# First tile's scores and row maxima ahead of the branch, row sums in PSUM, and a new order: windowed attention with two MoE layers on one core

## Chip, cores and metric

One core of a Trainium2 chip runs the whole program. The metric is device time in microseconds (us) of one execution. TensorE (the matmul engine) is PE in the profile, VectorE is DVE, ScalarE is ACT, GpSimd is POOL, SyncE is SP.

## What is computed

Sixteen attention heads (2 batches of 8; 768 rows, 64 wide) with 4 sink columns and a window of 128, then two feed-forward layers on the 1536 x 512 result.

```
scores = q @ k.T / sqrt(D)
keep = is_sink | in_window
a = exp(where(keep, scores, -1e9) - row max); a = a / (sum(a) + 1e-9)
x = a @ v
h = x @ w_in;  g = where(h >= 1, h, where(h <= -1, 0, (h + 1)**2 / 4));  x = g @ w_out
x = sigmoid(x @ w_gate) * (x @ w_val) @ w_out2
```

Sinks and window are inputs, so the program has two arms: a banded one for sizes that fit (these do), and a dense one for the rest. The arm is taken by a branch on a flag that the engines load into registers.

## The kernel before

Attention goes by tiles of 112 query rows, 7 per batch, 14 in all; each tile has four slots of two heads. Every slot takes the steps of `slot` in `banded`: PE makes the scores of both heads into a PSUM bank (`scores`, L922); DVE adds the mask and takes the row maximum in one custom instruction (`top`, L925); ACT takes the exponential and, with an accumulator read after it, the row sum (`exp`, L931); PE transposes the result (`turn`, L939); ACT or DVE copies it to SBUF as pts (`take`, helper line L353 or L355); PE multiplies with v (`values`, L962), all four slots of a tile together, into one bank. At the end of a tile DVE adds 1e-9 to the sums and inverts them (`inverse`, L976 and L977), the inverse is widened into ie, PE spreads it by four transposes (`spread`, L985), and the product is written as a high and a low float32r half (xh and xl) for the MoE layers. The first tile of a batch has only 128 key columns, the others 256.

The MoE matmuls are three per product (high by high, high by low, low by high): L550 to L552 for the first layer's input side, L595 to L597 for its output side, L712 and L798 to L800 for the second layer. Their weights arrive as int64 pieces through st, are put together by ACT and DVE (w), and split into halves.

A planner (`Plan.order`) sets the order of every engine's queue: it takes steps with costs, due times (`SLOT_DUE`, `FINISH`, `MOE_DUE` and others) and biases, and appends on each engine the step that is due first among those that can run. `Plan.fillers` puts matmuls of the identity (`fill`, L349) where it expects PE to stand idle in the first 55 us. The order is fixed when the program is built.

Ahead of the branch, in `moe_chain_kernel`: SP loads the sizes (nw) and the first tile's q and k, ACT issues the loads of its v and loads its exponential table (L1203); PE runs six warm matmuls (L1208); POOL tests the sizes (`banded_test`, its last step L1106 writes the flag); DVE makes the first mask. All engines then read the flag (L1212, L1213). The second tile's q and k are asked for behind the branch (L874).

The DMA loads take turns on eight semaphores: a load that reuses one waits, on the queue that issues it, until the load that used it before has landed.

Of the kernel before, what the change touches and what calls it, by code (L numbers as in the profile page):

```python
# [11 lines left out]
F32 = mybir.dt.float32  # L12
# [6 lines left out]
P = 128  # L19
# [33 lines left out]
START = {"DVE": 0.2}  # L53

BIAS = {"DVE": 0.31, "POOL": -0.06, "ACT": -0.05}

SLOT_DUE = 2.36

FINISH = {"top": 8.3, "exp": 5.74, "turn": 12.73, "pts": 8.44, "values": -10.81, "div": 8.03, "out": -13.31}
MOE_DUE = 62.74  # L60
MOE_PACE = 3.69
DRAIN = 1.91
EARLY = 18.59
LATE = 15.13
# [4 lines left out]
FIRST_TOPS = 4  # L69
SAME_MODE = 5.77  # L70
# [61 lines left out]

class Op:
# [3 lines left out]
class Plan:  # L137
# [40 lines left out]
    def order(self):  # L178
# [12 lines left out]
        done, events, now, order, mode = 0, [0.0], 0.0, [], None  # L191
# [106 lines left out]
class Body:  # L298


    def __init__(self, ctx, tc, a, out, pre):
# [17 lines left out]
        self.banks = [None] * 8  # L319
# [48 lines left out]

    def open_banks(self):
        ps = self.pool(self.ctx, "ps", True)  # L370
        self.psum = [ps.tile([P, 512], F32, name=f"bank{i}") for i in range(len(self.banks))]
# [467 lines left out]
    def banded(self):  # L839
# [3 lines left out]
        self.open_banks()  # L843
# [21 lines left out]
        def slot(k, due):  # L865
# [19 lines left out]
            if t == 0:  # L885
                v, rv = (lambda: first), cells("acc", 0, c0 - P, c0)
                op("SP", 0.0, -99.0, lambda: None, [], rq, lat=0.0)
                op("SP", 0.0, -99.0, lambda: None, [], rv, lat=2.0 + 0.2 * p)
# [8 lines left out]
            if j == 0:  # L897
                sc = [Buf(sc_r) for _ in range(2)]
# [3 lines left out]
            pr, mx, pt, pts = Buf(pr_r), Buf(mx_r), Buf(pt_r), Buf(pts_r)  # L902
# [21 lines left out]
            def top(e):  # L924
                nc.vector.tensor_tensor_reduce(  # L925
                    out=pr.ap[:n, e, :ks * P], in0=banks[e].ap[:n, j, :ks * P], in1=mask[:n, :ks * P], op0=ALU.add, op1=ALU.min,
                    scale=-0.125, scalar=3.0e38, accum_out=mx.ap[:n, e:e + 1],
                )
# [13 lines left out]
            yield 0.43 * f, scores, rq, [(x, j) for x in sc], sc  # L942
            for e in range(2):
                tops.append(op("DVE", d2_us(m) + 0.01, due - FINISH["top"], lambda e=e: top(e), [(banks[e], j), ("mask", min(i, 2))], [(pr, e), (mx, e)], uses=[banks[e], pr, mx]))
            for e in range(2):
                op("ACT", a_us(m) + 0.185, due - FINISH["exp"], lambda e=e: exp(e), [(mx, e)], [(pr, e), (sums, 2 * p + e)], uses=[pr, mx, sums])
            op("PE", 0.38 * f + 0.02, due - FINISH["turn"], turn, [(pr, 0), (pr, 1)], [pt], uses=[pr])

# [20 lines left out]
            if p == NP - 1:  # L969
# [22 lines left out]
                op("DVE", 0.28, due - FINISH["div"], inverse, [(sm, h) for h in range(H)], [sm], port=True)  # L992
# [16 lines left out]
        for k in range(0, len(slots), NP):  # L1009
            if k == NP:  # L1010
                op("DVE", 1.25, SLOT_DUE * (NP - 2), masks.make_second, [], [("mask", 1)], after=tops[:FIRST_TOPS])
# [3 lines left out]
            for j in range(0, NP, SCORES_OF):  # L1015
# [12 lines left out]
    def dense(self):  # L1028
# [5 lines left out]
        with ExitStack() as ctx:  # L1034
            ap, pp = self.pool(ctx, "dense"), self.pool(ctx, "dps", True)
            t = lambda shape, tag, dt=F32: ap.tile(shape, dt, tag=tag, name=tag)
            for b, p in [(b, p) for b in range(self.B) for p in range(NP)]:
# [5 lines left out]
                for i in range(S // P):  # L1043
# [11 lines left out]
                    ot = pp.tile([P, P], F32, tag="ot", name="ot")  # L1055
                    for e in range(2):
                        es = slice(64 * e, 64 * e + 64)
                        sc = pp.tile([P, 2, 512], F32, tag="sc", name="sc")
                        for c in range(2):
                            cs = slice(c * half, (c + 1) * half)  # L1060
                            for n, (x, y) in enumerate(((qh, kh), (qh, kl), (ql, kh))):
                                nc.tensor.matmul(out=sc[:, c, :half], lhsT=x[es, :], rhs=y[es, cs], start=n == 0, stop=n == 2)
                        pr, sm = t([P, S], "pr"), t([P, 4], "sm")
                        for c in range(2):
                            cs = slice(c * half, (c + 1) * half)
                            nc.vector.scalar_tensor_tensor(out=pr[:, cs], in0=sc[:, c, :half], scalar=0.125, in1=keep[:, cs], op0=ALU.mult, op1=ALU.mult)
# [7 lines left out]
                        pt, pts = pp.tile([P, 8, P], F32, tag="pt", name="pt"), t([P, nk, P], "pts")  # L1074
                        for c in range(nk):
                            nc.tensor.transpose(out=pt[:, c, :], in_=pr[:, c * P:(c + 1) * P], identity=ident)
                        nc.scalar.activation(out=pts, in_=pt[:, :nk, :], func=AF.Copy)
# [4 lines left out]
        self.open_banks()  # L1082

    def split(self, v, hi, lo):
        self.nc.scalar.activation(out=hi, in_=v, func=AF.Copy)
        self.nc.vector.tensor_tensor(out=lo, in0=v, in1=f32v(hi), op=ALU.subtract)


def banded_test(nc, const, nf):
# [10 lines left out]
    banded = const.tile([1, 1], F32, name="banded")  # L1100
# [20 lines left out]
class Masks:  # L1121
# [27 lines left out]
    def make_first(self):  # L1149
# [4 lines left out]
        self.weigh(m0)  # L1154
# [10 lines left out]
    def make_others(self):  # L1165
# [3 lines left out]
        v.tensor_copy(out=even[:, P:], in_=odd[:, :P])  # L1169


@with_exitstack
def moe_chain_kernel(ctx: ExitStack, tc: tile.TileContext, a, out):
# [12 lines left out]
    with tc.manual_schedule():  # L1186
# [18 lines left out]
        with tc.tile_pool(name="warm", bufs=1, space=bass.MemoryType.PSUM) as warm:  # L1205
            w = warm.tile([P, P], F32, name="warm")
            for i in range(WARM):
                nc.tensor.matmul(out=w, lhsT=pre["ident"], rhs=pre["ident"], start=i == 0, stop=i == WARM - 1)  # L1208
        pre["masks"] = Masks(nc, const, nf, pre["acc"])
        banded = banded_test(nc, const, nf)  # L1210
        pre["masks"].make_first()
        on = nc.values_load(banded[0:1, 0:1], min_val=0, max_val=0x3F800000)  # L1212
    with tc.If(on > 0) as branch:  # L1213
# [77 lines left out]
```

## Time and profile before

| | |
|---|---|
| median of 3 runs | 631.98 us (631.81 to 632.01) |
| profiled execution | 631.99 us |
| its span, first to last instruction | 630.2 us |
| busy: PE, DVE, ACT, POOL | 620.8, 498.8, 320.6, 160.1 us |
| mean granted clock of PE, share of full | 0.996 |

The profiled execution lies within 0.01 us of the median. Busy times are sums over stages with different limits, so the stretches have to be read apart: attention up to about 116 us, the first MoE layer mixed into it and after it, then the second. Matmuls overlap, and a busy PE may be busy with filler matmuls.

### The profile page before, as it was taken

How to read it: one execution, taken by the hardware profiler on the slowest of the kernel's cores; microseconds unless marked ns; L12 is line 12 of the kernel's file. 1: busy time of each engine (PE TensorE's matmuls, PEld its weight loads, DVE VectorE, ACT ScalarE, POOL GpSimd, SP SyncE). 2: the span in 40 equal slices, each digit the busy share in tenths (PEclk: the TensorE clock that was granted, in tenths of full speed). 3: DMA queues.
4: the chain of work that ended last, by engine and by line, in shares of the span. 5: the costliest groups of instructions: out<-in, count | busy, mean ns of one | idle time of the engine just before them, and what ended most of it. 6: DMA issues, size and time to landing. Idle time of an engine off the chain costs nothing.

```text
span 630.2 us, 9870 instructions
## 1 busy us (share of the span) xinstructions
PE 620.8 (99%) x3540; PEld 541.9 (86%) x3540; DVE 498.8 (79%) x1034; ACT 320.6 (51%) x736; POOL 160.1 (25%) x187
## 2 busy tenths in 40 slices
PE   7999999999999999999999999999999999999996
PEld 6778878888888888888888999998998998998995
DVE  4999998699996984459967697599789789786373
ACT  5999999646532531134435565663353442541430
POOL 1113411312000130025142323252351361460100
PEclk8999999999999999999999999999999999999999
DMA  6785655142441210001300001221212202200004
GB/s 186 255 260 179 177 174 185 47 153 82 154 147 67 70 65 33 1 0 34 124 11 0 1 34 67 101 68 67 100 36 71 97 34 100 69 1 0 1 35 172
DMA packets 28571, 54.48 MB, mean 86 GB/s; under 512 B 3296, under 2 KB 18400, under 8 KB 28512
## 3 DMA queue, kind: packets, MB, share of 16 engines
q1 hardware_dynamic: 27936, 53.49, 25.6%
q8 instruction: 30, 0.49, 0.3%
q10 hardware_dynamic: 576, 0.26, 0.1%
q14 instruction: 29, 0.24, 0.1%
HBM read 50.60 MB, written 3.15 MB: 85 GB/s over the span
## 4 chain that ended last, share of the span: by engine, by line
PE 95%; DVE 3%; DMA 1%; issue 0%; POOL 0%; ACT 0%
PE bank L712 28%; PE bank L550 7%; PE bank L595 7%; PE bank L596 7%; PE bank L597 7%; PE bank L551 7%; PE bank L552 7%; PE bank L800 5%; PE bank L799 5%; PE bank L798 5%; PE bank L922 3%; PE bank L962 3%; PE bank L939 3%; DVE pr L925 1%; PE bank L349 1%; PE bank L985 1%
## 5 line engine op out<-in xcount | busy, mean ns | idle before, releaser
L712 PE MATMUL bank<-xh,early 128*128 128x384 f32 x384 | 108.2, 334 | 0.0
L712 PE MATMUL bank<-late,early 128*128 128x384 f32 x432 | 85.5, 335 | 0.0
L712 PEld LDWEIGHTS bank<-late,early 128*128 128x128 f32 x432 | 76.1, 188 | 0.6
L712 PEld LDWEIGHTS bank<-xh,early 128*128 128x128 f32 x384 | 70.3, 188 | 0.4
L353 ACT ACTIVATE early<-w 128x512 fp32r<-128x512 f32 (+1 forms) x52 | 30.2, 582 | 68.5 <-PE bank L800 28.1
L712 PE MATMUL bank<-xl,early 128*128 128x384 f32 x192 | 64.2, 334 | 0.0
L808 DVE TENSOR_TENSOR acc<-bank,acc 128x512 f32<-128x512 f32 (+1 forms) x61 | 41.6, 681 | 21.5 <-PE bank L800 21.0
L569 ACT ACTIVATE tmp<-tmp 128x512 f32<-128x512 f32 x48 | 30.0, 629 | 52.2 <-DVE tmp L566 52.2
L931 ACT ACTIVATE pr<-pr,mx 112x256 f32<-112x256 f32 (+2 forms) x112 | 54.0, 488 | 4.3 <-DVE mx L925 4.2
L465 DVE SCALAR_TENSOR_TENSOR w<-st,w 128x512 int32<-128x512 int32 x68 | 51.0, 753 | 0.3
L462 DVE SCALAR_TENSOR_TENSOR w<-st,w 128x512 int32<-128x512 int32 x68 | 50.4, 743 | 0.8
L611 DVE TENSOR_TENSOR acc<-bank,acc 128x512 f32<-128x512 f32 x36 | 24.4, 688 | 29.1 <-PE bank L597 29.1
L405 POOL TENSOR_TENSOR w<-w 128x256 f32<-128x256 f32 x48 | 41.5, 876 | 21.7 <-DVE w L465 11.1
L566 DVE TENSOR_SCALAR tmp<-bank 128x512 f32<-128x512 f32 x48 | 32.7, 686 | 13.3 <-PE bank L552 12.8
L451 ACT ACTIVATE w<-st 128x512 f32<-128x512 f32 x60 | 39.3, 663 | 6.7 <-DMA st<-in_w 2.5
L353 ACT ACTIVATE gs<-tmp 128x512 fp32r<-128x512 f32 (+1 forms) x49 | 30.3, 621 | 23.7 <-DVE tmp L572 22.2
L925 DVE CUSTOM_DVE_ANT_0 pr<-bank,mask 112x256 f32<-112x256 f32 (+2 forms) x112 | 39.2, 396 | 3.6 <-PE bank L922 3.3
L360 DVE TENSOR_TENSOR early<-w,early 128x512 fp32r<-128x512 f32 x45 | 33.9, 758 | 7.4 <-POOL early L357 6.3
L456 DVE TENSOR_SCALAR w<-w 128x512 f32<-128x512 f32 x68 | 35.6, 526 | 5.2 <-ACT w L451 5.2
L360 POOL TENSOR_TENSOR early<-w,early 128x512 fp32r<-128x512 f32 (+1 forms) x25 | 27.0, 1083 | 46.7 <-ACT early L353 34.3
L550 PE MATMUL bank<-xh,early 128*128 128x512 f32 x96 | 38.3, 399 | 0.3 <-DVE mx L925 0.3
L595 PE MATMUL bank<-gs,early 128*128 128x512 f32 x96 | 38.0, 396 | 0.0
(170 smaller groups left out, 1557.1 us busy)
## 6 DMA issues: line engine op xcount, KB each, us to landing
st<-in_w SPq DMA_DIRECT2D x32, 512.0 KB, 3.3
v<-in_vb SPq DMA_DIRECT2D x52, 128.0 KB, 2.9
qk<-in_qk SPq DMA_DIRECT2D x48, 128.0 KB, 3.2
st<-in_wg SPq DMA_DIRECT2D x12, 512.0 KB, 3.3
st<-in_wv SPq DMA_DIRECT2D x12, 512.0 KB, 3.3
st<-in_wo SPq DMA_DIRECT2D x12, 512.0 KB, 3.2
out<-acc SPq DMA_DIRECT2D x11, 256.0 KB, 2.1
acc<-in_qk SPq DMA_DIRECT2D x12, 128.0 KB, 3.1
```

Source lines behind the costliest of these rows:

```text
L353: self.nc.scalar.activation(out=out, in_=x, func=AF.Copy)
L360: (self.nc.vector if e == "DVE" else self.nc.gpsimd).tensor_tensor(out=out, in0=x, in1=y, op=ALU.subtract)
L462: nc.vector.scalar_tensor_tensor(out=t(), in0=high(), scalar=-0x80000000, in1=t(), op0=ALU.bitwise_and, op1=ALU.bitwise_or)
L465: nc.vector.scalar_tensor_tensor(out=t(), in0=low(), scalar=29, in1=t(), op0=ALU.logical_shift_right, op1=ALU.bitwise_or)
L550: mm(out=out, lhsT=wh[:, c], rhs=mh, start=k == 0, stop=False)
L551: mm(out=out, lhsT=wh[:, c], rhs=ml, start=False, stop=False)
L552: mm(out=out, lhsT=wl[:, c], rhs=mh, start=False, stop=k == KD - 1)
L595: mm(out=out, lhsT=wh[:, c], rhs=gh, start=f == fs[0], stop=False)
L596: mm(out=out, lhsT=wh[:, c], rhs=gl, start=False, stop=False)
L712: nc.tensor.matmul(out=out, lhsT=w[:, c], rhs=m, start=start and i == n == 0, stop=i == 1 and n == 2, skip_group_check=True)
L925: nc.vector.tensor_tensor_reduce(out=pr.ap[:n, e, :ks * P], in0=banks[e].ap[:n, j, :ks * P], in1=mask[:n, :ks * P], op0=ALU.add, op1=ALU.m ...
L931: nc.scalar.activation(out=pr.ap[:n, e, :ks * P], in_=pr.ap[:n, e, :ks * P], func=AF.Exp, bias=mx.ap[:n, e:e + 1], scale=-1.0, accum_out=s ...
```

## The change

The program gets eight PSUM banks at its start. Ahead of the branch, PE now makes the scores of the whole first tile (L1244) and DVE its masked rows and maxima (the new helper `row_tops`, L1188), into a free piece of acc and a small tile mx0. The q and k of the first two tiles and the v of the first are loaded ahead of the branch, by SP and ACT in turn. POOL's test ends after two subtractions, and DVE makes the flag from them in one instruction (L1122); the branch compares it with the bit pattern of 1.0. The row sums of the exponentials go into eight spare columns of the bank that later takes the tile's values, and `inverse` reads them there. The planner's numbers are new. In the dense arm, which doesn't run here, the banks are the shared ones; that part and other small edits are left out below.

```diff
-START = {"DVE": 0.2}
+START = {"ACT": 0.9, "DVE": 2.1, "PE": 1.0, "SP": 1.1}
...
-SLOT_DUE = 2.36
+SLOT_DUE = 3.32
...
-SAME_MODE = 5.77
+SAME_MODE = 0.06
...
             if t == 0:
                 v, rv = (lambda: first), cells("acc", 0, c0 - P, c0)
...
-                load(own, src(i), due - 6, held(t) if t < RAW else [mine])
+                if t > 1:
+                    load(own, src(i), due - 6, held(t) if t < RAW else [mine])
...
+            total = lambda o: self.psum[o.bank][:, NP * TQ:NP * TQ + 2 * NP]
 
             def exp(e):
                 nc.scalar.activation(
                     out=pr.ap[:n, e, :ks * P], in_=pr.ap[:n, e, :ks * P], func=AF.Exp,
-                    bias=mx.ap[:n, e:e + 1], scale=-1.0, accum_out=sums.ap[:n, 2 * p + e:2 * p + e + 1],
+                    bias=mx.ap[:n, e:e + 1], scale=-1.0, accum_out=total(o)[:n, 2 * p + e:2 * p + e + 1],
                 )
...
-            yield 0.43 * f, scores, rq, [(x, j) for x in sc], sc
+            if t:
+                yield 0.43 * f, scores, rq, [(x, j) for x in sc], sc
...
-                    nc.vector.tensor_scalar(out=x[:, 1], in0=x[:, 0], scalar1=1e-9, scalar2=None, op0=ALU.add)
+                    nc.vector.tensor_scalar(out=x[:, 1], in0=total(o)[:n], scalar1=1e-9, scalar2=None, op0=ALU.add)
...
-    v.tensor_tensor(out=a, in0=a, in1=b, op=ALU.mult)
-    v.tensor_scalar(out=a, in0=a, scalar1=0.0, scalar2=None, op0=ALU.is_ge)
-    v.tensor_tensor(out=a[:, :2], in0=a[:, :2], in1=a[:, 2:], op=ALU.mult)
-    v.tensor_tensor(out=banded, in0=a[:, :1], in1=a[:, 1:2], op=ALU.mult)
-    return banded.bitcast(I32)
+    return a, b
+
+
+def banded_flag(nc, const, fits):
...
+    nc.vector.tensor_tensor_reduce(out=a, in0=a, in1=b, op0=ALU.mult, op1=ALU.max, scale=-1.0, scalar=0.25, accum_out=flag)
+    return flag.bitcast(I32)
...
+def row_tops(nc, out, x, mask, top):
+    nc.vector.tensor_tensor_reduce(out=out, in0=x, in1=mask, op0=ALU.add, op1=ALU.min, scale=-0.125, scalar=3.0e38, accum_out=top)
...
-        for p in range(min(KD, NP)):
-            c0 = p * NT + S - TQ - 2 * NS
-            nc.sync.dma_start(out=pre["acc"][:, c0:c0 + NQK], in_=a["qk"][0, 0, p])
+        pairs = [(p, p * NT + S - TQ - 2 * NS, (nc.sync, nc.scalar)[p % 2]) for p in range(NP)]
+        for p, c0, queue in pairs:
+            queue.dma_start(out=pre["acc"][:, c0:c0 + NQK], in_=a["qk"][0, 0, p])
+        for p, c0, queue in pairs:
+            queue.dma_start(out=pre["acc"][:, c0 + NQK:c0 + 2 * NQK], in_=a["qk"][0, 1, p])
+        for p, c0, queue in pairs:
             v = pre["acc"][:, c0 - P:c0]
-            nc.scalar.dma_start(out=v, in_=a["vb"][0, 0, p, :, 1])
+            queue.dma_start(out=v, in_=a["vb"][0, 0, p, :, 1])
...
+        masks.make_first()
+        flag = banded_flag(nc, const, fits)
+        masks.weigh(masks.first)
...
+        for p, c0, _ in pairs:
+            for e in range(2):
+                x = pre["acc"][64 * e:64 * e + 64, c0:c0 + NQK]
+                nc.tensor.matmul(out=first[e][:, p], lhsT=x[:, :TQ], rhs=x[:, TQ + NS:], start=True, stop=True)
+        for p in range(NP):
+            for e in range(2):
+                row_tops(nc, rows(p)[:, e], first[e][:, p], masks.first, pre["mx"][:, 2 * p + e:2 * p + e + 1])
+        on = nc.values_load(flag[0:1, 0:1], min_val=0, max_val=0x7F800000)
+    with tc.If(on < FIRST_FLAG) as branch:
```

PE's queue, from the flag on. Before (L922 scores of the first tile, L349 fillers, L939 transposes):

```order
L1212 TENSOR_LOAD banded
L1213 COMPARE_AND_BRANCH
L922 MATMUL bank_160<-acc 112x128
...
L349 MATMUL bank_165<-ident 128x128 x5
L939 MATMUL bank_164<-ident,pr 128x112 x2
L349 MATMUL bank_160<-ident 128x128
L939 MATMUL bank_165<-ident,pr 128x112 x2
L349 MATMUL bank_160<-ident 128x128 x4
L922 MATMUL bank_166<-acc 112x256
```

And now (L1244 scores of the first tile, L927 of the second, L943 transposes, L970 values, L354 fillers, L993 the spread):

```order
L1244 MATMUL bank_98<-acc 112x128
...
L1248 TENSOR_LOAD flag
L1249 COMPARE_AND_BRANCH
L927 MATMUL bank_93<-acc 112x256
...
L943 MATMUL bank_97<-ident,acc 128x112 x2
L943 MATMUL bank_98<-ident,acc 128x112 x2
...
L970 MATMUL bank_92<-pts,acc 64x112 x8
L354 MATMUL bank_93<-ident 128x128 x3
L993 MATMUL bank_99<-ident,ie 128x112 x4
```

The first tile's scores have moved ahead of the flag, the second tile's stand right behind it in one group of eight, and three fillers stand behind the first tile's values. Before, ten stood between the first tile's scores and the second's.

ACT's queue from its start. Before (L931 exponentials, L353 copies):

```order
L1196 DMA acc<-in_vb 128x128 x4
L1203 ACT_TABLE_LOAD
L1203 ACTIVATE scratch<-ident 1x1
L1212 TENSOR_LOAD banded
L1213 COMPARE_AND_BRANCH
L931 ACTIVATE pr,sm<-pr,mx 112x128 x4
L353 ACTIVATE pts<-bank_164 128x2x112
L931 ACTIVATE pr,sm<-pr,mx 112x128
L353 ACTIVATE pts<-bank_165 128x2x112
L931 ACTIVATE pr,sm<-pr,mx 112x128 x3
L353 ACTIVATE ie<-sm 112x512
```

And now (L935 exponentials, L358 copies):

```order
L1213 DMA acc<-in_qk 128x256 x2
L1215 DMA acc<-in_qk 128x256 x2
L1218 DMA acc<-in_vb 128x128 x2
L1225 ACT_TABLE_LOAD
L1225 ACTIVATE scratch<-ident 1x1
L1248 TENSOR_LOAD flag
L1249 COMPARE_AND_BRANCH
L935 ACTIVATE acc,bank_92<-acc,mx_131 112x128 x8
L358 ACTIVATE pts<-bank_97 128x2x112
...
L935 ACTIVATE pr,bank_98<-pr,mx 112x256 x4
```

Two more DMA issues stand ahead of the table load, all eight exponentials of the first tile stand ahead of its four copies of pts, each writes its sum to a bank, and the copy of ie has left this stretch.

PE in two later tiles, before:

```order
L922 MATMUL bank_160<-qk_177 112x256
...
L939 MATMUL bank_165<-ident,pr 128x112 x4
L939 MATMUL bank_163<-ident,pr 128x112 x4
L922 MATMUL bank_166<-qk_185 112x256
...
L985 MATMUL bank_167<-ident,ie 128x112 x4
L939 MATMUL bank_161<-ident,pr 128x112 x4
L962 MATMUL bank_165<-pts,v 64x112 x16
```

And now:

```order
L927 MATMUL bank_92<-qk_198 112x256
...
L927 MATMUL bank_98<-qk_190 112x256
...
L943 MATMUL bank_93<-ident,pr 128x112 x4
L943 MATMUL bank_99<-ident,pr 128x112 x4
L993 MATMUL bank_92<-ident,ie 128x112 x4
L943 MATMUL bank_93<-ident,pr 128x112 x4
L943 MATMUL bank_94<-ident,pr 128x112 x4
L970 MATMUL bank_97<-pts,v 64x112 x16
```

Two groups of four score matmuls, with transposes between them, have become one group of eight, and the spread stands ahead of the values as before. Over the whole attention the order has 20 groups of scores before and 16 behind the branch now.

## Rows read from the trace of the kernel before

**Rows 1.** The page's first part: busy us, share of the span, instructions.

```profile
PE 620.8 (99%) x3540; PEld 541.9 (86%) x3540; DVE 498.8 (79%) x1034; ACT 320.6 (51%) x736; POOL 160.1 (25%) x187
```

**Rows 2.** Windows: stretch, length, busy by engine (instructions), PE clock, DMA share, GB/s.

```profile
20.00:50.00 30.00, 29.74 (x318) 22.93 (x315) 29.78 (x123) 29.61 (x102) 3.96 (x6) 1.00 0.76 247
50.00:100.00 50.00, 49.42 (x468) 40.50 (x468) 49.42 (x161) 47.98 (x155) 15.34 (x18) 1.00 0.61 185
```

**Rows 3.** PE's waits behind its first matmuls: us in total, times, longest.

```profile
PE bank L939 <- DVE mx L925: 0.3, 1, 0.3
PE bank L939 <- ACT pts L353: 0.3, 1, 0.3
PE bank L550 <- DVE mx L925: 0.3, 1, 0.3
```

**Rows 4.** Timeline of PE, 6 to 17 us: start, us, operation, count, idle before.

```profile
6.33 1.13 PE L922 MATMUL bank<-acc 64*112 64x128 f32 x16 [2.05 <-POOL banded L1106]
7.39 2.20 PE L349 MATMUL bank<-ident 128*128 128x128 f32 x10
9.39 0.58 PE L939 MATMUL bank<-ident,pr 112*128 112x112 f32 x2
...
10.59 1.35 PE L349 MATMUL bank<-ident 128*128 128x128 f32 x8
...
13.36 0.40 PE L349 MATMUL bank<-ident 128*128 128x128 f32 x2
13.60 0.55 PE L985 MATMUL bank<-ident,ie 112*128 112x112 f32 x4
14.08 1.12 PE L922 MATMUL bank<-acc 64*112 64x256 f32 x8
...
16.96 1.98 PE L922 MATMUL bank<-acc 64*112 64x256 f32 x16
```

**Rows 5.** Timeline of ACT, SP and POOL (q: the queue issues), to 14 us.

```profile
0.72 1.86 ACTq L1196 DMA_DIRECT2D acc<-in_vb  x4
...
2.62 1.28 ACT L1203 ACT_TABLE_LOAD   x1 [2.62 <-issue]
...
3.86 0.33 SPq L1194 DMA_DIRECT2D acc<-in_qk  x1
...
5.23 0.18 POOL L1106 TENSOR_TENSOR banded<-fits 1x1 f32<-1x1 f32 x1
...
7.53 0.40 ACT L931 ACTIVATE pr<-pr,mx 112x128 f32<-112x128 f32 x1 [3.42 <-DVE mx L925]
7.84 0.18 ACT L931 ACTIVATION_READ_ACCUMULATOR pr<-pr,mx 112x1 f32 x1
7.93 0.39 ACT L931 ACTIVATE pr<-pr,mx 112x128 f32<-112x128 f32 x1
...
13.86 0.51 ACT L931 ACTIVATE pr<-pr,mx 112x256 f32<-112x256 f32 x1
```

**Rows 6.** What SP's queue waited for: us in total, times, longest.

```profile
SPq L1194 <- DMA acc<-in_vb: 1.3, 1, 1.3
```

**Rows 7.** Timeline of DVE: the second mask's first and last step, a maximum.

```profile
8.83 0.28 DVE L1158 TENSOR_SCALAR mask<-acc,nf 112x128 f32<-112x128 f32 x1
...
9.87 0.29 DVE L1147 TENSOR_SCALAR mask<-mask 112x256 f32<-112x256 f32 x1
...
13.02 0.42 DVE L925 CUSTOM_DVE_ANT_0 pr<-bank,mask 112x256 f32<-112x256 f32 x1 [0.24 <-PE bank L922]
```

**Rows 8.** Groups of ACT by form: busy us, mean ns of one, idle before.

```profile
L353 ACT ACTIVATE bank<-bank 128x384 f32<-128x384 f32 x48 | 22.9, 476 | 13.7 <-PE bank L712 13.2
L931 ACT ACTIVATION_READ_ACCUMULATOR pr<-pr,mx 112x1 f32 x96 | 18.6, 194 | 0.0
...
L353 ACT ACTIVATE tmp<-bank 128x384 f32<-128x384 f32 x24 | 11.7, 486 | 7.6 <-PE bank L712 7.4
```

**Rows 9.** Windows again, 8 to 10 us.

```profile
8.00:10.00 2.00, 2.00 (x11) 2.00 (x11) 1.97 (x16) 1.18 (x7) 0.00 (x0) 0.50 0.89 253
```

More of the change, by code (lines that the diff above doesn't have):

```diff
@@ L52 @@
 DMA_LAT = 2.7
-START = {"DVE": 0.2}
-BIAS = {"DVE": 0.31, "POOL": -0.06, "ACT": -0.05}
-SLOT_DUE = 2.36
[L59 to L64, printed above, removed]
+START = {"ACT": 0.9, "DVE": 2.1, "PE": 1.0, "SP": 1.1}
+READY = {"tops": 0.2, "next": 0.5, "values": 1.5}
+BIAS = {"DVE": 0.92, "POOL": 0.54, "ACT": 0.39}
+SLOT_DUE = 3.32
+FINISH = {"top": 3.98, "exp": 6.33, "turn": 10.24, "pts": 21.57, "values": -3.1, "div": -2.85, "out": -20.08}
+MOE_DUE = 126.14
+MOE_PACE = 8.22
+DRAIN = 2.91
+EARLY = 31.49
+LATE = 44.63
 ENTER, LEAVE = {"rows": 0.18, "cols": 0.14}, 0.09
@@ L68 @@
 VALUES_OF = 4
-FIRST_TOPS = 4
-SAME_MODE = 5.77
+SAME_MODE = 0.06
 WARM = 6
@@ L130, in __init__ @@
         ring.asked.append(self)
+class Kept:
+    def __init__(self, ap):
+        self.ap = ap
 class Op:
@@ L190, in order @@
                     ready[e].append((0.0, o))
-        done, events, now, order, mode = 0, [0.0], 0.0, [], None
+        done, events, now, order, mode = 0, sorted({0.0, *START.values()}), 0.0, [], None
         running = []
@@ L924, in top @@
             def top(e):
[L925 to L928, printed above, removed]
+                row_tops(nc, pr.ap[:n, e, :ks * P], banks[e].ap[:n, j, :ks * P], mask[:n, :ks * P], mx.ap[:n, e:e + 1])
+            total = lambda o: self.psum[o.bank][:, NP * TQ:NP * TQ + 2 * NP]
             def exp(e):
@@ L991, in slot @@
                 m = NP * n
-                op("DVE", 0.28, due - FINISH["div"], inverse, [(sm, h) for h in range(H)], [sm], port=True)
+                op("DVE", 0.28, due - FINISH["div"], inverse, [(sm, h) for h in range(H)], [sm], port=True, uses=[o])
                 pool = t >= POOL_FROM
@@ L1010, in banded @@
             if k == NP:
-                op("DVE", 1.25, SLOT_DUE * (NP - 2), masks.make_second, [], [("mask", 1)], after=tops[:FIRST_TOPS])
+                op("DVE", 1.25, SLOT_DUE * (NP - 2), masks.make_second, [], [("mask", 1)])
             if k == 2 * NP:
@@ L1014, in banded @@
             tile = [slot(k + j, SLOT_DUE * (k + j)) for j in range(NP)]
-            for j in range(0, NP, SCORES_OF):
+            for j in range(0, NP if k else 0, SCORES_OF):
                 both(tile[j:j + SCORES_OF], SLOT_DUE * (k + j), "rows")
@@ L1061, in dense @@
                             for n, (x, y) in enumerate(((qh, kh), (qh, kl), (ql, kh))):
-                                nc.tensor.matmul(out=sc[:, c, :half], lhsT=x[es, :], rhs=y[es, cs], start=n == 0, stop=n == 2)
+                                nc.tensor.matmul(out=sc[c][:, :half], lhsT=x[es, :], rhs=y[es, cs], start=n == 0, stop=n == 2)
                         pr, sm = t([P, S], "pr"), t([P, 4], "sm")
@@ L1065, in dense @@
                             cs = slice(c * half, (c + 1) * half)
-                            nc.vector.scalar_tensor_tensor(out=pr[:, cs], in0=sc[:, c, :half], scalar=0.125, in1=keep[:, cs], op0=ALU.mult, op1=ALU.mult)
+                            nc.vector.scalar_tensor_tensor(out=pr[:, cs], in0=sc[c][:, :half], scalar=0.125, in1=keep[:, cs], op0=ALU.mult, op1=ALU.mult)
                         nc.vector.tensor_tensor(out=pr, in0=pr, in1=fill, op=ALU.add)
@@ L1073, in dense @@
                         nc.vector.tensor_scalar(out=pr, in0=pr, scalar1=sm[:, 3:4], scalar2=None, op0=ALU.mult)
-                        pt, pts = pp.tile([P, 8, P], F32, tag="pt", name="pt"), t([P, nk, P], "pts")
+                        pts = t([P, nk, P], "pts")
                         for c in range(nk):
-                            nc.tensor.transpose(out=pt[:, c, :], in_=pr[:, c * P:(c + 1) * P], identity=ident)
-                        nc.scalar.activation(out=pts, in_=pt[:, :nk, :], func=AF.Copy)
+                            x = pt[c // 4][:, c % 4 * P:(c % 4 + 1) * P]
+                            nc.tensor.transpose(out=x, in_=pr[:, c * P:(c + 1) * P], identity=ident)
+                        for c in range(0, nk, 4):
+                            m = min(4, nk - c)
+                            nc.scalar.activation(out=pts[:, c:c + m].rearrange("p c n -> p (c n)"), in_=pt[c // 4][:, :m * P], func=AF.Copy)
                         for c in range(nk):
@@ L1204, in moe_chain_kernel @@
         pre["scratch"] = scratch
[L1205 to L1213, printed above, removed]
+        ps = ctx.enter_context(tc.tile_pool(name="ps", bufs=1, space=bass.MemoryType.PSUM))
+        pre["psum"] = [ps.tile([P, 512], F32, name=f"bank{i}") for i in range(8)]
+        for i in range(WARM):
+            nc.tensor.matmul(out=pre["psum"][0][:, :P], lhsT=pre["ident"], rhs=pre["ident"], start=i == 0, stop=i == WARM - 1)
+        pre["masks"] = masks = Masks(nc, const, nf, pre["acc"])
+        fits = banded_test(nc, const, nf)
+        masks.make_first()
+        flag = banded_flag(nc, const, fits)
+        masks.weigh(masks.first)
+        pre["mx"] = const.tile([TQ, 2 * NP], F32, name="mx0")
+        pre["pr"] = [pairs[p // 2][1] + 3 * NQK + p % 2 * 2 * P for p in range(NP)]
+        rows = lambda p: pre["acc"][:TQ, pre["pr"][p]:pre["pr"][p] + 2 * P].rearrange("p (e n) -> p e n", e=2)
+        pre["rows"] = rows
+        first = [pre["psum"][6 + e][:TQ].rearrange("p (i n) -> p i n", i=NP) for e in range(2)]
+        for p, c0, _ in pairs:
[7 more added lines that the diff above has]
+    with tc.If(on < FIRST_FLAG) as branch:
         with tc.manual_schedule(), ExitStack() as arm:
```

38 lines of the change are left out of this document (20 added, 18 removed).

## The prediction, made before the changed kernel ran

> **What bounds the kernel now.** I read four views in this order. The page's first part [rows 1] has TensorE (PE) busy for 620.8 of 630.2 us, so time can come from two places only: from what PE does that is no work, and from the few us in which it does nothing. The windows by stretch [rows 2] say where the other engines could stop PE: from 20 to 100 us DVE and ACT are as full as PE (ACT 29.6 of 30 us, then 48.0 of 50; DVE 29.8 and 49.4). The list of PE's waits [rows 3] shows how little is lost later: three waits of 0.3 us, 0.9 together. The timeline of PE's first 17 us [rows 4] shows the rest: it stands for 2.05 us before its first matmul behind the branch, and from 7.39 to about 11.9 it does little but filler matmuls (L349, identity by identity), while ACT's exponentials go on and the second tile's q and k, which are asked for only after the branch, are on their way. So the start is a chain through DMA, DVE and ACT that PE covers with fillers; from about 14 us on PE, ACT and DVE are all full; after the attention PE alone counts.
>
> **What the change takes off PE.**
> First, the first tile's scores. Their 16 records run from 6.33 to 7.39 [rows 4], behind the branch; now they stand ahead of it, in time in which PE waited. 1.06 us off.
> Second, fillers. The old order has 13, two records each. Ten records take 2.00 us (7.39 to 9.39), eight 1.35, two 0.24 (13.36 to 13.60) [rows 4]; the six others I put at 0.9. Together 4.5 us. The new order has four: three behind the first tile's values and one later. One costs between 0.24 and 0.40 by the same rows; I take 0.3, 1.2 us. 3.3 us off.
> Third, regrouping. Four score matmuls last 1.12 us and eight last 1.98 [rows 4], so a group of scores costs some 0.2 us beside its work. Without the first tile the old order has 19 such groups and the new one 16; with an estimated 0.1 us for the switch ahead of each, and for each of three switches fewer from MoE matmuls into the attention, 1.2 us are off.
> Fourth, the branch. The flag was POOL's last step, 5.23 to 5.41, and PE's first matmul came 0.92 us later [rows 4, 5]. Now DVE makes it in one step in place of POOL's last four, at about 4.9 us. But PE has scores ahead of its flag read, and their q and k must land: ACT's first load, issued at 0.72, landed when SP's fourth issue could go, at 3.86 [rows 5, 6], so those issued by 1.7 us land up to 4.8. PE is through its scores at about 5.3 and passes the branch at about 6.2, 0.1 us earlier.
> Together 5.7 us.
>
> **What it adds.** Two waits.
> ACT's queue now issues six DMAs where it issued four in 1.86 us, and loads its exponential table behind them (1.28 us) [rows 5]. The fifth and sixth reuse the semaphores of ACT's own first two loads, and SP's fourth issue waited 1.3 us for such a landing [rows 6]. So ACT's fifth goes at about 3.9 us, the sixth ends near 4.8, the table near 6.1, and with the small activation and the branch the first exponential starts at about 6.6, against 7.53 [rows 5]. Eight exponentials of the first tile at 0.39 us and four copies of pts at about 0.25 end at 10.7, where the second tile's exponentials can start: 3.1 us before the 13.86 of now. PE meanwhile does the second tile's scores (6.2 to 8.1) and has then eight transposes and eight values (about 0.8 and 0.9 us) until 11.2. That leaves 1.4 us in which it waits, in place of fillers.
> The values now also wait for DVE: the sums lie in the bank that the values write, and DVE's reading of them must be over first. In the new order it stands behind four maxima of the second tile. DVE ends the first tile's maxima at about 6.9 (at 8.83 now [rows 7]), is through the branch at 7.6, needs 1.3 us for the second mask (8.83 to 10.16) and 1.6 for four maxima of 0.42 at most, and has read the sums by about 10.8: 0.1 us more for PE. In the later tiles PE's spread of the reciprocals mostly stands ahead of the values and waits for a later DVE or POOL step anyway: nothing.
> So 1.5 us come back. The 0.9 us of waits I leave as they are.
>
> **The row sums in PSUM.** No row shows ACT's accumulator written there. Its read lasts 194 ns, and the next exponential starts 0.09 us after the read began (7.84 to 7.93) [rows 5, 8]. The nearest row is a copy of 384 columns that ends in PSUM, 476 ns against 486 into SBUF [rows 8]: 0.01 us off each of 112, 1.1 us of ACT. As one end I take 0.04 us each (four times that row, 4.5 us of ACT); at the other the overlap is lost, 0.10 us more each and 11.2 us of ACT. I take 0.01, by the nearest row. Being ACT time, it pays PE nothing directly; it and seven ie copies fewer on ACT (now DVE's and POOL's) let ACT keep up with a PE that has 5.7 us less to do. The copies moved to POOL I cost at nothing: PE has transposes ahead of the spread. Without that cover PE waits for each.
>
> **The sum.** The profiled execution took 631.99 us (span 630.2 and 1.8 around it); the median of the runs is 631.98. 631.99 - 5.7 + 1.5 = **627.8 us**. With the filler price and the wait in the ramp at their ends, 626.4 to 629.2.
>
> **A rule that speaks against it.** From 8 to 10 us the granted clock was 0.50, that is 1.2 GHz [rows 9], after PE had stood for 2.05 us ahead of its first matmul; after more fillers and work it was 2.4 GHz (1.00 from 20 us on [rows 2]). The change takes fillers out of just this stretch, but fills the hole ahead of the branch in part. The Trainium skill (TensorE: Matmul & The Clock Gate, What's actually happening) says that the throttled state is the default and that activity releases it. By that rule the new wait behind 8.1 us could bring a slow stretch of its own; the rival below gives its time from rows.
>
> **The rivals.**
> *No wait in the ramp.* ACT could read the flag while its table loads and start at 6.0, and the fillers may fall where PE waits. Then the 1.5 us don't come back, and some of the 0.9 goes: 626.0.
> *ACT and DVE set the pace.* Up to the last attention matmul the new order has 36 MoE matmuls fewer on PE to fill in with, and DVE takes over some xl and ie work from POOL and ACT. From 20 to 100 us ACT had 2.4 us to spare and DVE 0.8 [rows 2]. If PE must wait 2 us more for them in the later tiles: 629.8. For it speaks that all three are full, against it the ACT time saved.
> *The clock falls late.* If it is at half from about 11 to 14.5 us, the 2.5 us of values, transposes and scores there take twice as long: 630.3.
> *It doesn't do what it says.* If ACT's queue is another microsecond late and PE's scores wait longer for their landings, the start is as long as now, and the regrouping alone pays 0.3 us: 631.7.
> *Slower: the accumulator.* If a PSUM destination loses the overlap, each exponential takes 0.10 us more, 11.2 us of ACT; behind its 2.4 us of idle time 8.8 us reach PE: 636.6. From 0.07 us each on (7.8 less 2.4 is 5.4, more than the 4.2 gained) it is slower than now. The only row against it is the copy into PSUM, which is no longer than the one into SBUF.
>
> **How the numbers follow.** Forecast 0.48; no wait in the ramp 0.13; ACT and DVE 0.17; clock 0.09; no effect 0.05; slower 0.08. A measurement of this kernel can tell 0.2%, 1.26 us, from no change. Faster by more: all of the first two, 0.14 of the third and 0.07 of the fourth, 0.82. Within it: the rest of these and no effect, 0.10. Slower: 0.08. The range from 625.5 to 630.5 takes in the first two, most of the third and the clock, and leaves out some 0.17.
>
> **What would show it.** Right: PE's first matmul behind the branch near 6.2 us and the second tile's; the first exponential near 6.6, the second tile's near 10.7; four fillers; some 1.5 us of PE waiting for ACT or DVE between 8 and 12 us and about 1 us after that; accumulator reads of about 185 ns; PE's last attention matmul some 12 us earlier than now (4.2 and 36 MoE matmuls). Wrong: accumulator reads that hold up the next exponential by 0.16 us or more, the clock at 0.5 beyond 12 us, or several us of PE waits between 20 and 160 us.

## The result, and the profile after

The changed kernel takes 638.75 us (median of 5 runs), the kernel before 631.98: slower, by a ratio of 1.0118 (95% interval 1.0104 to 1.0132). The forecast was 627.8. Below is the windows view of the changed kernel, in the columns of [rows 2].

```profile
20.00:50.00 30.00, 27.35 (x316) 21.77 (x316) 25.52 (x110) 29.28 (x96) 3.32 (x5) 1.00 0.70 216
50.00:100.00 50.00, 47.64 (x450) 37.25 (x446) 46.07 (x160) 47.09 (x148) 13.77 (x17) 1.00 0.60 184
```

Before, PE, DVE and ACT were about equally full in these 80 us [rows 2]. Now, from 20 to 50 us, ACT alone is: it is busy for 29.28 of 30 us, PE for 27.35 (29.74 before) and DVE for 25.52 (29.78). From 50 to 100 us none of the three is (PE 47.64, ACT 47.09, DVE 46.07 of 50). So PE and DVE wait. PE's list of waits (columns of [rows 3]; its two largest and the next on ACT):

```profile
PE bank L943 <- ACT pts L358: 2.5, 5, 0.6
PE bank L993 <- DVE mx L1188: 1.7, 2, 1.0
...
PE bank L927 <- ACT on L358: 0.5, 1, 0.5
```

What makes ACT full is seen in ACT's timeline (start, us, operation):

```profile
4.76 1.04 ACTq L1218 DMA_DIRECT2D acc<-in_vb  x2
5.84 1.28 ACT L1225 ACT_TABLE_LOAD   x1 [5.84 <-DMA acc<-in_qk]
7.13 0.20 ACT L1225 ACTIVATE scratch<-ident 1x1 f32<-1x1 f32 x1
7.75 0.40 ACT L935 ACTIVATE acc<-acc,mx 112x128 f32<-112x128 f32 x1 [0.42 <-DVE mx L1188]
...
13.29 0.51 ACT L935 ACTIVATE pr<-pr,mx 112x256 f32<-112x256 f32 x1
13.70 0.15 ACT L935 ACTIVATION_READ_ACCUMULATOR pr<-pr,mx 112x1 f32 x1
13.89 0.51 ACT L935 ACTIVATE pr<-pr,mx 112x256 f32<-112x256 f32 x1
14.30 0.15 ACT L935 ACTIVATION_READ_ACCUMULATOR pr<-pr,mx 112x1 f32 x1
14.49 0.51 ACT L935 ACTIVATE pr<-pr,mx 112x256 f32<-112x256 f32 x1
14.90 0.15 ACT L935 ACTIVATION_READ_ACCUMULATOR pr<-pr,mx 112x1 f32 x1
14.96 0.56 ACT L358 ACTIVATE on<-bank 128x448 f32<-128x448 f32 x1
```

The accumulator read lasts 0.15 us where it lasted 0.19 [rows 8], but the exponential behind it starts 0.19 us after the read began (13.70 to 13.89); before it was 0.09 [rows 5]. So the exponential waits until the read has ended. A copy behind a read does not: it starts 0.06 after the read began (14.90 to 14.96). Over the whole trace, from the start of one 256-column exponential to the start of the one directly behind it is 0.599 us now (median of 63) and was 0.492 (median of 54); below this is called the step.

The start is less of a change than forecast. PE's timeline:

```profile
5.25 2.05 PE L1244 MATMUL bank<-acc 64*112 64x128 f32 x16 [0.97 <-DMA acc<-in_qk]
7.09 3.21 PE L927 MATMUL bank<-acc 64*112 64x256 f32 x16
10.23 0.70 PE L943 MATMUL bank<-ident,acc 112*128 112x112 f32 x5
11.22 0.32 PE L943 MATMUL bank<-ident,acc 112*128 112x112 f32 x1 [0.30 <-ACT acc L935]
11.99 0.41 PE L943 MATMUL bank<-ident,acc 112*128 112x112 f32 x2 [0.45 <-ACT pts L358]
```

The first tile's 16 score records stand ahead of the branch, as the change says, but they wait for q and k until 5.25 and take 2.05 us where they took 1.13 [rows 4]; the second tile's 16 take 3.21, where 16 such records took 1.98 [rows 4]. The first exponential comes at 7.75, no earlier than before (7.53 [rows 5]).

### The profile page after: what moved, and what is told of

The parts are those of the page before. It is cut to its first block, busy times and chain, and to the rows that moved or that the text cites. A ratio compares the mean times of both kernels' runs of the same rounds, so it can differ in the third digit from the quotient of the medians.

```text
span 636.7 us, 9882 instructions
## 1 busy us (share of the span) xinstructions
PE 623.1 (98%) x3522; PEld 541.2 (85%) x3522; DVE 502.9 (79%) x1045; ACT 330.4 (52%) x747; POOL 139.0 (22%) x163
## 4 chain that ended last, share of the span: by engine, by line
PE 84%; ACT 6%; DVE 6%; issue 2%; ACTq 0%
PE bank L713 27%; PE bank L596 7%; PE bank L598 7%; PE bank L597 7%; PE bank L553 6%; PE bank L551 6%; PE bank L552 6%; PE bank L801 5%; PE bank L800 5%; PE bank L799 5%; ACT pr L935 3%; ACT pts L358 2%; DVE pr L1188 2%; PE bank L970 1%; PE bank L943 1%
## 5 line engine op out<-in xcount | busy, mean ns | idle before, releaser
L713 PE MATMUL bank<-xh,early 128*128 128x384 f32 x384 | 106.1, 334 | 0.0
L358 ACT ACTIVATE early<-w 128x512 fp32r<-128x512 f32 (+1 forms) x62 | 36.4, 591 | 54.6 <-PE bank L713 30.7
L935 ACT ACTIVATE pr<-pr,mx 112x256 f32<-112x256 f32 (+2 forms) x104 | 51.9, 499 | 2.2
L406 POOL TENSOR_TENSOR w<-w 128x256 f32<-128x256 f32 x48 | 43.6, 919 | 42.2 <-DVE w L466 28.1
L466 DVE SCALAR_TENSOR_TENSOR w<-st,w 128x512 int32<-128x512 int32 x68 | 50.1, 739 | 0.4
L463 DVE SCALAR_TENSOR_TENSOR w<-st,w 128x512 int32<-128x512 int32 x68 | 48.9, 723 | 0.5
L358 ACT ACTIVATE gs<-tmp 128x512 fp32r<-128x512 f32 (+1 forms) x50 | 31.0, 622 | 26.4 <-DVE tmp L573 24.1
L365 DVE TENSOR_TENSOR early<-w,early 128x512 fp32r<-128x512 f32 x50 | 38.7, 778 | 7.5 <-ACT early L358 7.1
L551 PE MATMUL bank<-xh,early 128*128 128x512 f32 x96 | 38.2, 397 | 0.1
L596 PE MATMUL bank<-gs,early 128*128 128x512 f32 x96 | 37.9, 395 | 0.2 <-ACT pts L358 0.2
L553 PE MATMUL bank<-xh,early 128*128 128x512 f32 x96 | 37.4, 390 | 0.0
L597 PE MATMUL bank<-gs,early 128*128 128x512 f32 x96 | 37.4, 390 | 0.0
```

Of the source, the lines that this page charges most:

```text
L358: self.nc.scalar.activation(out=out, in_=x, func=AF.Copy)
L406: (self.nc.vector if e == "DVE" else self.nc.gpsimd).tensor_tensor(out=out, in0=x, in1=y, op=alu)
L463: nc.vector.scalar_tensor_tensor(out=t(), in0=high(), scalar=-0x80000000, in1=t(), op0=ALU.bitwise_and, op1=ALU.bitwise_or)
L466: nc.vector.scalar_tensor_tensor(out=t(), in0=low(), scalar=29, in1=t(), op0=ALU.logical_shift_right, op1=ALU.bitwise_or)
L551: mm(out=out, lhsT=wh[:, c], rhs=mh, start=k == 0, stop=False)
L553: mm(out=out, lhsT=wl[:, c], rhs=mh, start=False, stop=k == KD - 1)
```

## The experiments

Theory A: the eight row sums of a tile lie in one PSUM bank, so the program makes every exponential wait, on ACT's own semaphore, for the one before it, and that takes the overlap of neighbouring ACT instructions. Theory B: PSUM itself is the slow place for a row sum. Theory C: the new order or start costs the time. Ratios are to the kernel before, run beside each on the same chip, with the 95% interval.

**1. Sums back in SBUF.**

```diff
-accum_out=total(o)[:n, 2 * p + e:2 * p + e + 1]
+accum_out=sums.ap[:n, 2 * p + e:2 * p + e + 1]
-nc.vector.tensor_scalar(out=x[:, 1], in0=total(o)[:n], ...
+nc.vector.tensor_scalar(out=x[:, 1], in0=x[:, 0], ...
```

> The changed kernel with the exponentials' row sums written to the tile in SBUF again, and everything else as in the change: its start, its order, its held banks. Theory A (a wait: the eight sums of a tile lie in one PSUM bank, so each exponential waits for the one before it on ACT's own semaphore, about 0.11 us each, and 112 of them make ACT the bound of the ramp): the step from one 256-column exponential to the next falls from 0.60 to 0.49 us, the time by 7 to 10, to 629 to 632. Theory B (PSUM itself is the slow place for a row sum): the same here. Theory C (the new order or the new start costs the time, the sums do not): the time stays at 637 to 639.5.

631.86 us, ratio 0.9994 (0.9983 to 1.0005). C falls: the sums alone make 638.75 of 631.86, 6.9 us (by the two ratios, each to the runs beside it, 7.8). But without them the change brings nothing that can be measured. ACT's timeline has the old step again (12.31 to 12.81):

```profile
12.31 0.49 ACT L935 ACTIVATE pr<-pr,mx 112x256 f32<-112x256 f32 x1
12.71 0.19 ACT L935 ACTIVATION_READ_ACCUMULATOR pr<-pr,mx 112x1 f32 x1
12.81 0.49 ACT L935 ACTIVATE pr<-pr,mx 112x256 f32<-112x256 f32 x1
```

**2. Only the sums, in the kernel before.** The same lines the other way round, and the bank held from a tile's first exponential on (`uses=[pr, mx, sums, o]`, `uses=[o]` for the inverse).

> The kernel before with one part of the change: the row sums go to the free columns of the bank that takes the tile's values, and that bank is held from the tile's first exponential on. The planner's numbers and the start are those of before. Theories A and B: the step between exponentials rises to 0.60 us, 112 of them are 11 to 12 us of ACT, of which 5 to 9 reach the time: 637 to 641. Theory C: 631 to 633.

638.2 us, ratio 1.0089 (1.0072 to 1.0106), step 0.599. The sums cost 6 us in the old order too.

**3 and 4. Wait or place?** Run 3 takes the wait away and leaves PSUM; run 4 takes PSUM away and leaves the wait.

```diff
 # 3
-accum_out=total(o)[:n, 2 * p + e:2 * p + e + 1]
+accum_out=(total(o) if e == 0 else sums.ap)[:n, 2 * p + e:2 * p + e + 1]
 # 4
-accum_out=total(o)[:n, 2 * p + e:2 * p + e + 1]
+accum_out=sums.ap[:n, 0:1]
```

> The changed kernel with the sums of the first head of each pair in PSUM as in the change and those of the second head in SBUF as before (one more small instruction of DVE per tile reads them). The wait on ACT's own semaphore is then for the exponential before the last one. Theory A: that wait is over when it is asked, both kinds step by 0.49 us, time 629 to 632. Theory B: an exponential behind one with its sum in PSUM still starts 0.19 us after that one's accumulator read began, behind one with its sum in SBUF 0.09; half the loss stays, time 633 to 636. Theory C: 637 to 639.5.

> The changed kernel with all eight row sums of a tile written to one and the same column in SBUF (the division uses that one sum for all eight heads), so that each exponential waits for the one before it on ACT's own semaphore although no sum goes to PSUM. Theory A: the step stays at 0.58 to 0.60 us, time 636 to 640. Theory B: the step is 0.49 us, time 629 to 632. Theory C: 637 to 639.5.

Run 3: 631.58 us, 0.9992 (0.9982 to 1.0002). Run 4: 642.26 us, 1.0153 (1.0136 to 1.0171), step 0.634. Theory A is shown, B falls: with the wait and no PSUM the time is lost; with half of the sums in PSUM and no wait it is not. The traces name the wait: in the change and in run 4 all 75 exponentials that stand directly behind another carry a wait on the semaphore that ACT's own accumulator reads raise, and all of them start late; in run 3, where the sums of neighbours mostly lie apart, 27 of the 29 that carry one start early. ACT's timeline of run 3 says more than A expected:

```profile
12.24 0.16 ACT L935 ACTIVATION_READ_ACCUMULATOR pr<-pr,mx 112x1 f32 x1
12.29 0.51 ACT L935 ACTIVATE pr<-pr,mx 112x256 f32<-112x256 f32 x1
12.69 0.20 ACT L935 ACTIVATION_READ_ACCUMULATOR pr<-pr,mx 112x1 f32 x1
12.78 0.50 ACT L935 ACTIVATE pr<-pr,mx 112x256 f32<-112x256 f32 x1
```

Behind a read into PSUM the next exponential starts 0.05 us after it (12.24 to 12.29), behind one into SBUF 0.09 (12.69 to 12.78). So PSUM is the faster place by 0.04 us, as long as nothing waits: in run 3 the step is 0.450 behind a sum in PSUM and 0.491 behind one in SBUF (medians). In run 4 the step is longer than with the sums in PSUM, since the wait lasts until the read has ended and the read into SBUF is the longer one:

```profile
13.10 0.19 ACT L935 ACTIVATION_READ_ACCUMULATOR pr<-pr,mx 112x1 f32 x1
13.32 0.51 ACT L935 ACTIVATE pr<-pr,mx 112x256 f32<-112x256 f32 x1
```

**Where did the other savings go?** The ramp is here the stretch up to 100 us, in which PE, ACT and DVE are all nearly full. Theory D: ACT paces the ramp, and the time follows its first exponential. Theory E: PE's slow first scores (the "cold start") ate the gain. Theory F: the planner's wrong price for an exponential spoilt the order. Theory G, formed after run 8: DVE or PE holds the ramp as much as ACT; from run 16 on, ACT and DVE pace it by turns. All runs from here have their sums in SBUF, but run 7 (PSUM) and run 15 (as run 3).

**5. A warmer start.** `WARM = 10` for 6, and the first tile's v loaded by SP alone.

> The changed kernel with its row sums in SBUF (as in the first run) and a warmer start: ten warm-up products instead of six, so that TensorE doesn't idle before the first tile's q and k land, and the four loads of v of the first tile all on SP's queue, so that ACT's table load doesn't stand behind transfers. Theory D (the ramp is paced by ACT, which is busy 98 to 100% of 10 to 60 us; PE time saved there is refilled by waits): the second tile's 16 scores take 1.9 instead of 3.1 us, PE gains 1.5 to 2 us, and the time falls only by what ACT's first exponential comes earlier, 0.5 to 0.9: 630.9 to 631.4. Theory E (the cold start is what ate the gain): the time falls by all of it, to 629.5 to 630.3.

632.21 us, 1.0012 (1.0003 to 1.0022). PE's timeline:

```profile
5.92 1.53 PE L1244 MATMUL bank<-acc 64*112 64x128 f32 x16
7.29 1.89 PE L927 MATMUL bank<-acc 64*112 64x256 f32 x16
```

The second tile's scores take 1.89 us, 1.2 less, and nothing of it arrives. The first tile's scores came later, and the first exponential with them (7.88 for 7.64 in run 1), which is 0.24 us against the 1.2. E falls.

**6 and 7. The planner's price.** `a_us(m) + 0.185` with SBUF sums (6), and the true `a_us(m) + 0.295` with PSUM sums (7), in place of 0.141.

> The changed kernel with its row sums in SBUF and the planner told the exponential's cost of before (0.185 us on top of its columns instead of 0.141), so that it writes out another order by the same numbers. Theory D: waits move between engines, the time stays within 1 us of 631.9. If the planner's belief in a shorter exponential had spoilt the order (theory F), the time falls by 2 or more.

> The changed kernel with its row sums in PSUM as it is, and the planner told the step that the trace shows (0.295 us on top of the columns instead of 0.141). Theory A with D (the waits add 11 us to ACT, and ACT paces the ramp): no order can take them away, only move copies from ACT to DVE: 636 to 639.5. Theory F (the order is wrong for the durations, the durations themselves are harmless): 630 to 634.

631.7 us, 1.0007 (0.9997 to 1.0017), and 638.97 us, 1.0113 (1.0093 to 1.0133). F falls: neither of these two other orders gains anything.

**8. The table of numbers alone**, in the kernel before (BIAS to SAME_MODE of the change; start, branch and sums as before).

> The kernel before with one part of the change: the planner's table of numbers (due times, biases, the weight on staying in one mode) from the changed kernel; start, branch and row sums are those of before. Theory D: the new order trades fillers and switches of PE for waits on ACT and DVE, 631 to 634. By the forecast's terms for the order (fillers and regrouping, 4.5 us less 1.5 for waits) it should be near 629.

632.17 us, 1.0014 (1.0003 to 1.0026): the order that the new numbers give with the old start gains nothing either.

**9 and 10. Earlier row maxima.** The first tile's scores in banks 4 to 7 instead of 6 and 7, v of the first tile on SP alone, and in run 10 `WARM = 8`.

> The changed kernel with its row sums in SBUF, and two edits that let ACT's first exponential come earlier: the first tile's scores lie in four banks instead of two, so that the first row maximum waits for four products instead of sixteen, and the first tile's v is loaded by SP alone, so that ACT's table load is done before. TensorE's warm-up is left as it is (six products, cold second tile). Theory D (ACT paces the ramp, the time follows its first exponential): first exponential at 6.3 to 6.7 instead of 7.6 us, time 0.8 to 1.3 less than 631.9: 630.5 to 631.1. Theory E (PE's cold start is what counts): 631.5 to 632.2, since PE's start is not touched.

> The run before with eight warm-up products instead of six. Theory D: as the run before, within 0.4 us, for better if the scores come no later. Theory E: less by the 1.2 us that the second tile's scores lose cold.

632.56 us, 1.0008 (1.0000 to 1.0017), and 633.59 us, 1.0040 (1.0026 to 1.0055), with more spread than the others (631.0 to 636.5). The first exponentials came at 6.25 and 6.69, but SP's later loads stood behind the four of v. PE's waits in the profiled execution of run 9, at 636.53 us its slowest:

```profile
PE bank L927 <- DMA qk<-in_qk: 1.7, 1, 1.7
PE bank L927 <- DMA acc<-in_qk: 1.2, 2, 1.0
```

The profiled execution of run 10, at 631.66 us its fastest, has no such waits. So these two decide nothing about D.

**11 and 12. Half of every exponential**, in run 1's kernel and in the kernel before; the second half of each row is left without it.

```diff
-out=pr.ap[:n, e, :ks * P], in_=pr.ap[:n, e, :ks * P], func=AF.Exp,
+out=pr.ap[:n, e, :P], in_=pr.ap[:n, e, :P], func=AF.Exp,
```

> The changed kernel with its row sums in SBUF, and every exponential over the first 128 of its columns only (96 of 112 have 256), which takes 0.107 us off each, 10.3 us of ACT. The second half of each row is left without exponential. Theory D: with ACT no longer full, the forecast's savings on PE come out: the time falls by 3 to 6, to 626 to 629. If DVE or PE itself paces the ramp as much (theory G): it falls by 0 to 2, to 630 to 632.

> The kernel before with the same half exponentials (the second half of each row is left without exponential). PE had no holes in the ramp there, so under theory D ACT's relief brings less than in the changed kernel: the time falls by 0 to 2.5, to 629.5 to 632, and the changed kernel's order with SBUF sums is then the faster one by 2 to 5. Theory G: both stay at 630 to 632 and alike.

630.11 us, 0.9973 (0.9964 to 0.9982), and 631.53 us, 0.9997 (0.9988 to 1.0006). Ten us off ACT bring 1.8, which is what G expected; D alone is too little.

**13 to 15. The early maxima without the late loads.** As run 9, but v on both queues as in the change, and ACT's table load issued ahead of its loads of v; 14 with `WARM = 8`, 15 with the sums as in run 3.

> The early row maxima again (first tile's scores in four banks, row sums in SBUF), without the fault of that run: v of the first tile goes back to the two queues it has in the change, and ACT's table load is issued ahead of ACT's two loads of v, so SP's later loads stand behind nothing new. First exponential at 6.3 to 6.7 us. If the time follows ACT's first exponential while no load is late (theory D): 630.5 to 631.2. If an earlier ACT only waits later for DVE or PE (theory G): 631.5 to 632.2.

> The run before with eight warm-up products, so that TensorE is busier before the first q and k land. Theory E (PE's cold start costs): 0.5 to 1.2 less than that run. Theories D and G: within 0.4 of it.

> The first of these three with the sums of the first head of each pair in PSUM and those of the second in SBUF. The read of a sum that goes to PSUM was 0.03 us shorter, and no exponential has to wait for the one just before it: ACT has 56 times 0.03 = 1.7 us less, DVE 14 small instructions of 0.07 = 1.0 us more. Theory D: 0.2 to 0.8 less than the first of the three; theory G: the same within 0.4.

631.79 us, 0.9998 (0.9989 to 1.0007); 631.43 us, 0.9989 (0.9980 to 0.9998); 631.09 us, 0.9984 (0.9975 to 0.9993). In run 13 the first exponential started at 7.02, not at 6.3 as expected, which is 0.6 earlier than in run 1, and brought 0.1; the intervals of the two are too wide to rule out 0.6. Together with run 11 this speaks against D. In run 14 the second tile's scores take 2.06 us for the 3.16 of run 13, and the time is 0.4 less (0.6 by the ratios), at the edge of the 0.5 to 1.2 that E expected, so that a small part of E stays open. Run 15 is the fastest version that leaves nothing out; its interval leaves out "no change", but the gain is only about 1 us (0.16%).

**16 and 17. Half of DVE's maxima as well as of the exponentials**, in run 1's kernel and in the kernel before: `:P` for `:ks * P` in the row maxima too, and the transposes read that half twice, so that PE's work stays.

> The changed kernel with its row sums in SBUF, and both engines beside PE relieved: row maxima and exponentials over the first 128 columns only, and the transposes read that half twice, so that PE's work is as it was (the second half of each row is left out of the softmax). That takes 10.3 us off ACT and some 12 off DVE. Theory G (ACT and DVE pace the ramp by turns; the savings of the new order on PE are real but nothing feeds them): 626.5 to 629, 1 or more below the 630.1 that half exponentials alone gave. If PE itself holds the rest: 629.8 to 630.4.

> The kernel before with the same relief of both engines. PE had no holes there, so theory G expects 630.8 to 631.8, and the new order and start then worth 2.5 to 4.5 against it, what the forecast's terms for PE come to. If they are worth no more than the 1.4 that half exponentials alone showed, the forecast's terms for PE were themselves too large.

628.28 us, 0.9951 (0.9934 to 0.9968), and 631.61 us, 0.9995 (0.9986 to 1.0004). Windows of run 16, then of run 17:

```profile
20.00:50.00 30.00, 30.00 (x347) 24.93 (x347) 26.00 (x123) 28.68 (x113) 4.89 (x7) 1.00 0.82 268
50.00:100.00 50.00, 49.94 (x487) 41.23 (x486) 44.40 (x158) 42.86 (x147) 15.18 (x19) 1.00 0.57 173
```

```profile
20.00:50.00 30.00, 30.00 (x322) 23.27 (x320) 24.79 (x123) 26.96 (x100) 3.93 (x6) 1.00 0.78 248
50.00:100.00 50.00, 50.00 (x481) 41.26 (x479) 45.19 (x163) 44.90 (x158) 14.98 (x18) 1.00 0.62 189
```

With both neighbours relieved PE is full in both kernels, and the change without its sums in PSUM is worth 631.61 less 628.28, 3.3 us (2.8 by the ratios); with ACT alone relieved it was worth 631.53 less 630.11, 1.4. Run 1's own windows show what stood in its way: PE 29.10 of 30 us with ACT at 29.93, and then DVE at 9.93 of the 10 us from 60 to 70 while ACT falls to 8.95:

```profile
20.00:50.00 30.00, 29.10 (x335) 23.18 (x333) 27.84 (x116) 29.93 (x105) 4.33 (x7) 1.00 0.74 233
50.00:100.00 50.00, 49.01 (x458) 39.66 (x456) 47.51 (x165) 47.68 (x155) 15.17 (x20) 1.00 0.61 186
60.00:70.00 10.00, 9.15 (x93) 7.58 (x93) 9.93 (x36) 8.95 (x28) 3.66 (x5) 1.00 0.46 143
```

In run 1, PE's listed waits behind its first matmuls are nearly all at the spread (L993), and all of those are for DVE:

```profile
PE bank L993 <- DVE mx L1188: 1.3, 2, 0.8
PE bank L993 <- DVE ie L360: 0.4, 2, 0.3
PE bank L943 <- ACT pts L358: 0.3, 1, 0.3
```

In run 11 the two at the spread are down to 0.4 and 0.3, and in run 16 they are gone. So G fits all the runs: ACT and DVE hold PE by turns. Whether DVE alone would have given less than both was not tried, so that the turns are argued and not shown.

## Why the prediction was wrong

**The row sums in PSUM: the step that failed.** I took 0.01 us off each of 112 by the nearest row and gave the other end, overlap lost at 0.10 each, 0.08. Both of my ends came true at once. The place gains 0.04 us, the wait takes 0.15 (0.599 less the step of 0.450 in run 3), and 0.107 of loss is left. The sign of being wrong that I had named came true: a read holds up the next exponential by 0.19 us. In the change 75 exponentials stand directly behind another one: 75 times 0.107 is 8.0 us; 37 reads have another operation behind them and gain 0.04 each, 1.5. Together 6.5 us of ACT; 6.9 came out. I treated it as a question of the destination. The code held the answer: eight sums that used to be eight separate columns of an SBUF tile now share a bank, and the program guards a bank as a whole: separate columns of one bank wait (the change and run 2) as one shared column in SBUF does (run 4), and separate columns in SBUF don't (run 1). The Trainium skill (Perfetto Trace Analysis, Optimizing Scalar/DVE Operations) gives ScalarE's overhead of data access, per instruction, as about 93 ns on SBUF and about 51 on PSUM; the traces agree (from the start of a read to the next operation 0.093 us before and, where nothing waits, 0.051 in the change, medians). The same skill (PSUM — Partial Sum Buffer, PSUM bank collisions raise a hardware error) asks for a guard by bank between different engines; here both instructions are ACT's, and the wait between them is what cost the time.

**How much of it reaches PE.** The rival said 11.2 us of ACT less 2.4 of idle time. The 2.4 us took up nothing. Between run 1 and the change the whole of the addition arrives (6.5 of ACT, 6.9 of time), and between runs 1 and 4 too (75 times 0.142 is 10.7; 10.4 came out), although ACT is idle for 2.4 of the 80 us in run 1 as well (29.93 and 47.68 busy). In the old order it is the same: in run 2, 69 times 0.107 less 43 times 0.04 is 5.7 us of ACT, and 6 us came out. That rival's 636.6 lies near the result in part by luck: it had 4.7 us of ACT too much, which made up for most of the 2.4 of slack and of the 3.8 of other savings that did not come.

**Fillers, 3.3 us: the count was right.** 26 records of L349 with 5.6 us busy became 8 with 1.4; busy times of neighbours overlap a little, so 4.2 less busy is in line with 3.3. What the fillers alone take off the time no run shows.

**The first tile's scores, 1.06: mostly lost.** The next matmuls start at 7.09 instead of 7.39, 0.3 us. q and k came later than I took (5.25, not 4.8), and the scores took 2.05 us where [rows 4] has 1.13. But that need not be the change's doing: with the old start they take 2.05 in the traces of runs 2, 8, 12 and 17 as well (below run 17), so that the 1.13 belongs to the one trace that I read:

```profile
6.32 2.05 PE L922 MATMUL bank<-acc 64*112 64x128 f32 x16 [2.04 <-POOL banded L1106]
```

The rows do not show why the records are slow: the windows of the changed kernel read 1.00 for the granted clock from 4 to 8 us, but its trace has no entry of the clock before 9.7 us. From there to 100 us it is 1.00, so the rival of a late fall of the clock did not come true.

**The earlier second tile: too early.** Its 16 scores took 3.21 us where I took 1.98, and the first exponential came at 7.75, not 6.6: the table load ended near the time I gave plus a us (5.84 to 7.13), and the first maximum waited for the sixteen slow scores until 7.33. PE's waits for ACT between 8 and 12 us come to 0.75 us (0.30 and 0.45), half of the 1.5 that I gave.

**Regrouping, 1.2: not shown.** A group of 16 records lasts 0.2 us less than two of eight, so three groups fewer are 0.6; the rest was an estimate without a row, and no run has the regrouping alone.

**The sum against ACT and DVE.** Even with the sums right, the forecast's 4.2 us would not have come: run 1 has 0.4, which can't be told from nothing. Yet PE's own terms were near: with both neighbours relieved the change without its sums in PSUM is worth 3.3 us (runs 16 and 17), and PE's last matmul of the attention starts at 102.6 us in run 16 and at 115.0 in run 17, near the 12 us earlier that I gave. In the change it is 113.8, in run 1 107.0, in the kernel before 115.6. I had [rows 2], with all three engines full, and subtracted PE's savings as though PE alone counted. The spread's waits for DVE in the later tiles I had put at nothing; run 1 has 1.7 us of waits at the spread. The rival in which ACT and DVE set the pace, 629.8, had this mechanism (as far as G is right) and half of its size: run 1 lies 4.1 us above my 627.8, it said 2.

## What to carry to other kernels

Where a small result moves from separate columns of SBUF to one PSUM bank, ask first what the program's guard of that bank adds: look for waits of an engine on itself, and alternate the destinations so that no neighbours share a bank. Where three engines are full in the same stretch, work taken from one of them is worth, as these runs suggest, only what the other two can follow; relieve the neighbours artificially, as in runs 16 and 17, before trusting a sum for one engine. A rival whose price is 9 us deserves a look at the code that decides it, not just a chance of 0.08.

## What the runs showed of the hardware

An accumulator read with its destination in PSUM lets the next ACT operation start 0.05 us after it began, one in SBUF 0.09 (medians 0.051 in the changed kernel and 0.093 in the one before). A wait on ACT's own semaphore between two neighbouring exponentials costs 0.15 us with the sum in PSUM (a step of 0.599 after 0.450) and 0.14 in SBUF (0.634 after 0.492), since the next one starts only after the read has ended. Against sums in SBUF without a wait, as in the kernel before, the loss with PSUM is 0.107.
